# Other steps for the weight conversions beside an attention, other places for sums and remainders in the layers behind it

## The chip, the cores and the metric

The kernel runs on one core of a Trainium2 chip. Its time is the device time of one execution in microseconds, lower is better. Engines: PE is TensorE's matmul, PEld its weight load, DVE is VectorE, ACT is ScalarE, POOL is GpSimd, SP issues the DMAs. A conversion of a weight piece, a normalisation or a copy all run on one engine's queue in program order; an engine waits where an instruction's inputs or its output buffer are not free.

## The reference

Three layers follow each other. An attention (2 batches, 8 heads, 576 tokens, head size 64) with a bias that depends on positions, then a feed-forward layer, then 8 experts that are all computed for every token and summed with balanced weights.

```
scores = q @ k.T / 8 + bias[h, i, j]
attn = exp(scores - max) / sum;  x = attn @ v            # 1152 tokens x 512
h = x @ w_in;  g = softplus(h);  x = g @ w_out           # 512 -> 2048 -> 512
P = balanced(exp(x @ w_gate))                            # 8 rounds of rows and columns
out = sum over e of P[:, e] * (relu(x @ w1[e]) @ w2[e])  # 512 -> 1024 -> 512, e < 8
```

w_in and w_out arrive as 64 bit floats, everything else as 32 bit.

## The kernel before, in words

**The attention** walks over 8 pairs (batch, two heads). Each pair has nine steps, one for each tile of 128 query rows and head (five row tiles, some of them shared between the two heads). Step s runs 0 to 71; `r = s % 9` is the step's place in its round. In step s TensorE transposes the probabilities of step s - 3 (`transp`), computes the scores of step s + 1 (`qk`, two PSUM buffers) and multiplies older probabilities with v (`pv`), in an order that a table sets for each r. DVE adds the bias and takes the maximum (`soft`, L397), ACT takes the exponential (L401), and ACT or POOL normalises (`norm`, L409 and L411). `prep` makes the next pair's query and key operands in some of the steps (DVE casts at L293, POOL remainders at L332 and L343). At the end of each step `beside(s)` issues work of the next layer.

**Operands in two parts.** Matmuls run on a rounded high part and its remainder, three products for each: hi*hi, lo*hi, hi*lo. So every operand is split by one ACT copy and one subtraction on DVE or POOL. Weights: `parts` (L637 ACT, L638 POOL), called as "high" for a unit's up weights and "highd" for its down weights. Activations: L684, L660, L745 for the high part; L661, L747, L749 for the remainder.

**Conversions.** A piece of a 64 bit weight is loaded into a `raw` buffer and becomes 32 bit in a tile of `fs` in four steps: m (`rescale`, L602 ACT and L603 POOL), a (`convert_a`, L608 DVE), b (`convert_b`, L613 DVE), c (`convert_c`, L619 DVE). A unit has four pieces, two for the up weights, two for the down weights. For unit 0 the table EARLY gives, for each piece, the steps of its load, m, a, and b with c; ESPLIT the steps of "high" and "highd". Two `raw` buffers are there during the attention, so a piece's load waits for c of the piece two before it. For the later units a list (`todo`) is worked off by `convert(n)` in fixed places of the unit before.

**The units.** A unit is 256 columns of the hidden layer: the feed-forward layer has 8 (u < U1 = 8), the experts 32. A unit's up part makes z for two halves of 512 tokens (c) and two column blocks (f); 128 last tokens are computed apart (`up_last`, `turn_last`, `down_last`). Units 0, 1 and 8 do it plainly (`plain`, 12 matmuls for each z); the others by seven products in Strassen's manner (`product`, in the order 1, 2, 6, 5, 7, 3, 4), which need sums of the token blocks, S1 to S4 (`first_sum`, `first_split` in units 0 and 1), and sums of weights (`mix`). The products accumulate in three PSUM banks X ("t"), Y ("tail") and Z ("pv"); copies v1, u2, u3 keep what a bank held (`keep`, L729), and `add` (L724) makes z out of a bank and a copy. Then `act` or `rest_of` run softplus (L742, L777) and the split (L745, L747, L749). `down(u, c)` makes four chunks of tokens out of h and adds each to `acc` (`evac`, L848 on ACT in unit 0, L850 on DVE after it); acc lies in the buffers in which the attention's result x lay. `down_last` does it for the last tokens in the bank "pv", which product 5 of the next unit needs.

Z of unit 0's first two products lies in one PSUM tile of two banks (`pool["z"]`); DRAIN issues these products and the first softplus beside the last attention steps. The order of work on each engine is the program's own: nothing reorders it.

Of the kernel before, what the change touches and what calls it, by code (L numbers as in the profile page):

```python
# [70 lines left out]

EARLY = ((10, 14, 16, 19), (12, 20, 22, 25), (30, 36, 38, 41), (34, 42, 44, 47), (42,), (48,))
ESPLIT = ((28, "high", 0), (50, "highd", 0))
XAT = ((67, "A11", 0), (68, "A11", 1), (70, "A12", 0), (71, "A12", 1), (72, "A21", 0), (73, "A21", 1))

DRAIN = ((72, "up", (0, 0)), (74, "act", (0, 0)), (74, "up", (0, 1)))

# [15 lines left out]
def attention_moe_moe_kernel(ctx: ExitStack, tc, qT, kT, vN, wpos, w_in, w_out, w_gate, e_w1, e_w2,  # L93
# [439 lines left out]
    def experts(m0, accp, xr):  # L533
# [46 lines left out]
        def whole2(u, k):  # L580
            return fs[(0 if u == 0 else 3 + u % 2) if k else 2 * (u % 2)]

# [123 lines left out]

        def plain(u, c, f):

            if u == 0 and c == 0:
                if f == 0:  # L710
                    pool["z"] = ps2("z")
                zz = pool["z"][:, f]
            else:
                zz = bank(("t", "t", "tail", "pv")[2 * c + f] if u < U1 else "t")
            z[c, f] = zz
            for k in range(KT):
                for n, (a, b) in enumerate(TRIPS):
                    o = 256 * k + 128 * f
                    nc.tensor.matmul(zz, wu(u)[:, a, o:o + 128], xs[f"A{c + 1}{k // 2 + 1}"][b][k % 2],  # L719
                                     start=(k == 0 and n == 0), stop=(k == 3 and n == 2))  # L720

        def add(u, bank_, name):
            out = hold[bank_ if u >= U1 and name != "u3" else name]
            nc.vector.tensor_tensor(out=out, in0=hold[bank_], in1=hold[name], op=ALU.add)  # L724
            return out
# [28 lines left out]
        def low():  # L754
            while lows:
                lows.pop(0)()
# [313 lines left out]
        def unit(u):  # L1070
# [13 lines left out]
            if u < U1:  # L1084
# [4 lines left out]
                elif u in PLAIN:  # L1089
                    for n, (c, f) in enumerate(((0, 0), (0, 1), (1, 0), (1, 1))):  # L1090
                        do(u, (c, f))
                        low()
                        act(u, c, f, z[c, f])
                        if n == 1:
                            weights["highd"](u, 0)
                            first_split("S4")
                        convert(2)
                        jobs(n)
                    up_last(u)
                    low()  # L1100
                else:
                    for n, p in enumerate(UP):
# [13 lines left out]
                jobs(8)  # L1116
                turn_last(u)
                down(u, 1)
                if u == 0:
                    first_split("S2")  # L1120
                convert(len(todo))
                if u == 1:
                    first_split("S3", nc.vector)
                down_last(u)
                load_down()
# [60 lines left out]
        def first_plain():  # L1186

            def up(c, f):
                do(0, (c, f))
                low()  # L1190
                act(0, c, f, z[c, f])

            tmp = [pool["moe"].tile([128, 512], F32, tag=t, bufs=1, name=t) for t in ("v1", "u2", "u3", "s3")]
            pool["tmp"] = dict(S1=tmp[0:2], S2=[fs[1][:, 0:512], fs[1][:, 512:1024]], S3=tmp[2:4], S4=tmp[0:2])
            up(0, 0)
            first_sum("S1")
            low()
            first_sum("S2")
            up(0, 1)
            first_split("S1")  # L1200
            low()
            first_sum("S3")
            up(1, 0)
            first_sum("S4")
            up(1, 1)
            low()
            up_last(0)

# [132 lines left out]
```

## Time and profile before

| | |
|---|---|
| median of 3 runs | 1234.54 us (1233.07 to 1234.57) |
| the profiled execution's own time | 1233.09 us |
| its span, first to last instruction | 1231.3 us |
| mean granted TensorE clock | 0.992 |
| busy: PE, PEld | 96%, 81% |
| busy: DVE, ACT, POOL | 63%, 46%, 48% |

The position bias is built in the first 95 us; the attention's first bias add is at 100.3 us, its last at 258.5; unit 0's down part begins at 280, unit 2 at 319, the experts at 465. In the rows below times are counted from the span's start. A busy time is that of an engine's instructions; an idle time in brackets stands ahead of the instruction that it is printed with, and the name behind it is what the profile takes to have ended it.

### The profile page before, as it was taken

The numbers are of one execution on the slowest core, as the hardware profiler recorded it, in microseconds if no ns is written. First come the engines' busy times: TensorE is split into PE (matmuls) and PEld (weight loads), VectorE is DVE, ScalarE is ACT, GpSimd is POOL, SyncE is SP. The second block draws the span as 40 slices with busy tenths as digits, with TensorE's granted clock in tenths as the row PEclk, the third lists the DMA queues.
The fourth block names the chain that finished last, engine by engine and source line by source line (L and its number), as shares of the span: only waits on it lengthen the run. The fifth ranks groups of instructions, "written<-read, shape, count | busy, mean of one in ns | idle before, by whom it ended". The sixth has DMA issues, their size and how long they took to land.

```text
span 1231.3 us, 19016 instructions
## 1 busy us (share of the span) xinstructions
PE 1179.1 (96%) x7418; PEld 996.8 (81%) x7418; DVE 774.1 (63%) x1372; ACT 567.7 (46%) x987; POOL 591.5 (48%) x477
## 2 busy tenths in 40 slices
PE   5877999999999999999999999999999999999998
PEld 4776888888788877888888888888888888888887
DVE  8996778648888867466545555555554554554554
ACT  7976677767445554334334224224323323323421
POOL 0115676646787893434534534534533543543440
PEclk9898999999999999999999999999999999999999
DMA  3577566202222320111111111111111111111002
GB/s 101 169 209 209 171 194 181 83 35 87 86 73 100 103 69 18 52 35 52 52 35 52 52 35 45 58 36 35 54 50 35 52 52 35 52 52 35 35 1 77
DMA packets 58573, 90.86 MB, mean 74 GB/s; under 512 B 6900, under 2 KB 37236, under 8 KB 58484
## 3 DMA queue, kind: packets, MB, share of 16 engines
q1 hardware_dynamic: 58196, 89.35, 23.1%
q8 instruction: 58, 0.95, 0.3%
q10 hardware_dynamic: 288, 0.30, 0.1%
q14 instruction: 31, 0.25, 0.1%
HBM read 74.45 MB, written 15.19 MB: 73 GB/s over the span
## 4 chain that ended last, share of the span: by engine, by line
PE 84%; DVE 9%; ACT 3%; issue 1%; DMA 1%; POOL 1%; SPq 0%; DVEq 0%; POOLq 0%; ACTq 0%
PE sum L817 36%; PE t L703 15%; PE pv L703 8%; PE tail L791 4%; PE pv L833 4%; PE tail L703 4%; PE op L472 3%; PE sps L384 2%; PE tp L435 2%; PE t L719 1%; ACT m L197 1%; DVE m L200 1%; PE pac L210 1%; DVE extra L234 1%; DMA raw<-in_kT_dram 1%
## 5 line engine op out<-in xcount | busy, mean ns | idle before, releaser
L638 POOL TENSOR_TENSOR wu<-f,wu 128x1024 fp32r<-128x1024 f32 x77 | 186.3, 2419 | 410.1 <-ACT wu L637 409.3
L817 PE MATMUL sum<-wd,h 128*128 128x512 f32 x1536 | 364.7, 393 | 0.0
L817 PEld LDWEIGHTS sum<-wd,h 128*128 128x128 f32 x1536 | 283.3, 188 | 56.3
L852 DVE SCALAR_TENSOR_TENSOR acc<-sum,prob,acc 128x512 f32<-128x512 f32 x224 | 168.2, 751 | 146.5 <-PE sum L817 146.5
L703 PE MATMUL t<-room,wu 128*128 128x512 f32 x592 | 164.5, 389 | 0.0
L729 ACT ACTIVATE v<-t 128x512 f32<-128x512 f32 x37 | 22.2, 599 | 244.6 <-PE t L703 244.6
L703 PEld LDWEIGHTS t<-room,wu 128*128 128x128 f32 x592 | 111.1, 188 | 23.5 <-DVE u L724 0.3
L703 PE MATMUL pv<-x,wu 128*128 128x512 f32 x444 | 113.8, 392 | 2.5 <-DVE acc L850 2.4
L638 POOL TENSOR_TENSOR wd<-f,wd 128x1024 fp32r<-128x1024 f32 x40 | 96.5, 2414 | 11.3 <-ACT wd L637 10.5
L703 PEld LDWEIGHTS pv<-x,wu 128*128 128x128 f32 x444 | 82.6, 188 | 21.5 <-DVE acc L850 4.2
L637 ACT ACTIVATE wu<-f 128x1024 fp32r<-128x1024 f32 x77 | 81.0, 1053 | 29.9 <-POOL f L634 23.8
L210 PE MATMUL pac<-bw,m 128*128 128x64 bf16 (+1 forms) x1920 | 68.5, 200 | 27.2 <-ACT m L197 13.4
L817 PE MATMUL sum<-h,wd 128*128 128x512 f32 x384 | 91.6, 393 | 1.5 <-DVE h L749 0.8
L210 PEld LDWEIGHTS <-m 128*128 128x128 bf16 (+1 forms) x1920 | 65.2, 105 | 30.3 <-issue 17.7
L703 PE MATMUL t<-x,wu 128*128 128x512 f32 x296 | 85.1, 389 | 0.0
L817 PEld LDWEIGHTS sum<-h,wd 128*128 128x128 f32 x384 | 70.5, 188 | 17.1 <-ACT acc L848 1.5
L745 ACT ACTIVATE hl<-tail 128x256 fp32r<-128x256 f32 x40 | 15.5, 386 | 141.8 <-PE tail L800 141.8
L724 DVE TENSOR_TENSOR u<-t,u 128x512 f32<-128x512 f32 x37 | 25.6, 692 | 72.4 <-PE t L703 69.8
L850 DVE TENSOR_TENSOR acc<-sum,acc 128x512 f32<-128x512 f32 x80 | 55.0, 688 | 22.9 <-PE sum L817 22.1
L703 PEld LDWEIGHTS t<-x,wu 128*128 128x128 f32 x296 | 55.6, 188 | 11.5
L724 DVE TENSOR_TENSOR tail<-tail,v 128x512 f32<-128x512 f32 x31 | 21.7, 700 | 67.7 <-PE tail L703 67.7
L401 ACT ACTIVATE p<-p,sm 128x576 f32<-128x576 f32 x72 | 55.6, 772 | 17.4 <-DVE sm L397 14.4
(224 smaller groups left out, 2116.6 us busy)
## 6 DMA issues: line engine op xcount, KB each, us to landing
f<-in_e_w_dram SPq DMA_DIRECT2D x128, 256.0 KB, 2.8
bias<-wt SPq DMA_DIRECT2D x16, 576.0 KB, 5.8
raw<-in_w_in_dram SPq DMA_DIRECT2D x16, 512.0 KB, 3.6
raw<-in_w_out_dram SPq DMA_DIRECT2D x16, 512.0 KB, 3.5
wt<-extra SPq DMA_DIRECT2D x10, 512.0 KB, 4.4
raw<-in_qT_dram SPq DMA_DIRECT2D x16, 288.0 KB, 4.3
raw<-in_kT_dram SPq DMA_DIRECT2D x16, 288.0 KB, 4.4
vr<-in_vN_dram SPq DMA_DIRECT2D x8, 448.0 KB, 4.8
```

What stands on the lines that cost most here:

```text
L210: nc.tensor.matmul(pt[0:n, g], lhs, win(w, (k * (ng + 1) + gw) * NC, [[(ng - gw) * NC, 2], [1, NC]]), start=(k == 0), stop=(k == 2))
L401: nc.scalar.activation(p, p, AF.Exp, bias=sm[:, o:o + 1], scale=-1.0, accum_out=sm[:, 2 + o:3 + o])
L472: nc.tensor.matmul(op[:, 0:n], l, r, start=(part == 0 and k == 0), stop=(part == 8))
L637: nc.scalar.activation(w[:, 0], src, AF.Copy)
L638: nc.gpsimd.tensor_tensor(out=w[:, 1], in0=src, in1=w[:, 0].bitcast(F32), op=ALU.subtract)
L703: nc.tensor.matmul(zz, wu(u)[:, a, o:o + 128], xs[xn][b][j], start=(n in (1, 2, 5) and k == 0), stop=(k == 5), skip_group_check=True)
L724: nc.vector.tensor_tensor(out=out, in0=hold[bank_], in1=hold[name], op=ALU.add)
L791: nc.tensor.matmul(zr[:, 0:256], xl[:, b, k], wu(u)[:, a, 256 * k:256 * k + 256], start=(n == 0), stop=(n == 3 * KT - 1))
L817: nc.tensor.matmul(s, lhs, rhs, start=(n == 0), stop=(n == 5))
L833: nc.tensor.matmul(r, t[:, b, 128 * f:128 * f + 128], w[:, a, f], start=(n == 0), stop=(n == 5))
L850: nc.vector.tensor_tensor(out=d, in0=o, in1=d, op=ALU.add)
L852: nc.vector.scalar_tensor_tensor(out=d, in0=o, scalar=pool["prob"][:, t, e:e + 1], in1=d, op0=ALU.mult, op1=ALU.add)
```

## The change

1. EARLY: m, a, and b with c of unit 0's four pieces move to other steps, all four pieces to the same three places of a round (8, 2, 3). The last two pieces' loads move two steps ahead, unit 1's second one two steps back.
2. ESPLIT: "high" and "highd" of unit 0 move from steps 28 and 50 to 63 and 72. For that the down weights of unit 0 lie in `fs[1]`, no longer in the up weights' `fs[0]`.
3. DRAIN: the second z product is issued ahead of the first softplus.
4. Unit 0's plain products of c = 1 are cut into two halves of the contraction, A21's for both f, then A22's. S4 is summed behind the remainders of h, into `fs[0]`.
5. The splits of S1, S2 and S4 move: S1 from unit 0's up part to the end of unit 1's, S2 ahead of unit 0's second down half, S4 from the middle of unit 1 behind that half.
6. `down_last` comes ahead of the conversions that are left in `todo` (and ahead of the S3 split in unit 1).
7. `add`: in the feed-forward layer product 3's sum stays in the PSUM bank; before it went to the SBUF tile u2.

```diff
-EARLY = ((10, 14, 16, 19), (12, 20, 22, 25), (30, 36, 38, 41), (34, 42, 44, 47), (42,), (48,))
-ESPLIT = ((28, "high", 0), (50, "highd", 0))
+EARLY = ((10, 17, 20, 21), (12, 26, 29, 30), (28, 35, 38, 39), (32, 44, 47, 48), (42,), (50,))
+ESPLIT = ((63, "high", 0), (72, "highd", 0))
...
-DRAIN = ((72, "up", (0, 0)), (74, "act", (0, 0)), (74, "up", (0, 1)))
+DRAIN = ((72, "up", (0, 0)), (74, "up", (0, 1)), (74, "act", (0, 0)))
...
         def whole2(u, k):
-            return fs[(0 if u == 0 else 3 + u % 2) if k else 2 * (u % 2)]
+            return fs[(1 if u == 0 else 3 + u % 2) if k else 2 * (u % 2)]
...
-        def plain(u, c, f):
+        def plain(u, c, f, ks=range(4)):
...
-            else:
+            elif ks[0] == 0:
                 zz = bank(("t", "t", "tail", "pv")[2 * c + f] if u < U1 else "t")
+            else:
+                zz = z[c, f]
             z[c, f] = zz
-            for k in range(KT):
+            for k in ks:
...
         def add(u, bank_, name):
-            out = hold[bank_ if u >= U1 and name != "u3" else name]
+            out = hold[name if name == "u3" or (u < U1 and name == "v1") else bank_]
...
                         if n == 1:
                             weights["highd"](u, 0)
-                            first_split("S4")
                         convert(2)
                         jobs(n)
                     up_last(u)
                     low()
+                    first_split("S1")
...
                 turn_last(u)
+                if u == 0:
+                    first_split("S2")
                 down(u, 1)
                 if u == 0:
-                    first_split("S2")
+                    first_split("S4")
+                down_last(u)
                 convert(len(todo))
                 if u == 1:
                     first_split("S3", nc.vector)
-                down_last(u)
                 load_down()
...
             def up(c, f):
-                do(0, (c, f))
                 low()
                 act(0, c, f, z[c, f])
...
             up(0, 1)
-            first_split("S1")
+            for ks in ((0, 1), (2, 3)):
+                for f in range(2):
+                    plain(0, 1, f, ks)
             low()
             first_sum("S3")
             up(1, 0)
-            first_sum("S4")
             up(1, 1)
             low()
+            first_sum("S4")
             up_last(0)
```

Three places in the engines' rows show it. First DVE in the attention, around b and c (L613, L619) of unit 0's first piece; L397 is the bias add of a step, L415 a remainder of transposed probabilities, L421 a copy of them, L293 the cast of the next pair's keys. Before:

```order
L407 RECIPROCAL sm<-sm 128x1
L613 SCALAR_TENSOR_TENSOR f_2555<-raw_2557,f_2555 128x512
L619 SCALAR_TENSOR_TENSOR f_2555<-raw_2557,f_2555 128x512
L397 ISA p,sm<-sps,bias 128x576
L397 ISA sm 128x1
L421 COPY po<-tp 128x4x128
L421 COPY po<-tps 128x320
L406 TENSOR_SCALAR sm<-sm 128x1
```

And of the change:

```order
L415 TENSOR_TENSOR pt<-tp,pt 128x4x128
L407 RECIPROCAL sm<-sm 128x1
L613 SCALAR_TENSOR_TENSOR f_2555<-raw_2557,f_2555 128x512
L619 SCALAR_TENSOR_TENSOR f_2555<-raw_2557,f_2555 128x512
L397 ISA p,sm<-sps,bias 128x576
L397 ISA sm 128x1
L415 TENSOR_TENSOR pt<-tp,pt 128x4x128
L407 RECIPROCAL sm<-sm 128x1
L293 CAST ks<-raw 128x1152
```

The pair stood ahead of the bias add of the round's step 2; now it stands two bias adds later, ahead of that of step 4, behind which the key cast comes.

Next TensorE at the attention's end: z is unit 0's second product, op the last products with v, tail and pv unit 0's products of c = 1 (room is A21 and the high part of A22, x_4613 the remainder of A22). Before:

```order
L472 MATMUL op<-pt,vx 128x320 x6
L719 MATMUL z<-room,wu_2553 128x512 x12
L472 MATMUL op<-po,vr 128x320 x5
L719 MATMUL tail<-room,wu_2553 128x512 x7
L719 MATMUL tail<-x_4613,wu_2553 128x512
L719 MATMUL tail<-room,wu_2553 128x512 x2
```

And of the change:

```order
L472 MATMUL op<-pt,vx 128x320 x6
L721 MATMUL z<-room,wu_2553 128x512 x12
L472 MATMUL op<-po,vr 128x320 x5
L721 MATMUL tail<-room,wu_2553 128x512 x6
L721 MATMUL pv<-room,wu_2553 128x512 x6
L721 MATMUL tail<-room,wu_2553 128x512
L721 MATMUL tail<-x_4613,wu_2553 128x512
```

z keeps its place on TensorE (what moved is ACT's softplus, which is now issued behind it); twelve matmuls that need only A21 now stand ahead of the first that needs A22.

Last DVE at the end of unit 1: acc<-pv adds the last tokens, L608, L613 and L619 convert unit 2's last piece, L1220 is the S3 remainder, L724 the first z of unit 2. Before:

```order
L850 TENSOR_TENSOR acc<-sum,acc 128x512
L608 TENSOR_SCALAR f_4603<-f_4603 128x512
L613 SCALAR_TENSOR_TENSOR f_4603<-raw_4606,f_4603 128x512
L619 SCALAR_TENSOR_TENSOR f_4603<-raw_4606,f_4603 128x512
L1220 TENSOR_TENSOR room<-u_4631,room 128x512
L1220 TENSOR_TENSOR room<-s_4632,room 128x512
L850 TENSOR_TENSOR acc<-pv,acc 128x512
L724 TENSOR_TENSOR v_5014<-tail,v_5014 128x512
```

And of the change:

```order
L852 TENSOR_TENSOR acc<-sum,acc 128x512
L608 TENSOR_SCALAR f_4603<-f_4603 128x512
L852 TENSOR_TENSOR acc<-pv,acc 128x512
L613 SCALAR_TENSOR_TENSOR f_4603<-raw_4606,f_4603 128x512
L619 SCALAR_TENSOR_TENSOR f_4603<-raw_4606,f_4603 128x512
L1226 TENSOR_TENSOR room<-u_4631,room 128x512
L1226 TENSOR_TENSOR room<-s_4632,room 128x512
L726 TENSOR_TENSOR v_5014<-tail,v_5014 128x512
```

The add of the last tokens moved ahead of four instructions, not of the first of the three conversions; the first z of unit 2 stands behind the same work as before.

## Rows read from the trace of the kernel before

**Rows 1.** Windows, one round each: stretch, length, engines' busy us (count), clock, DMA share, GB/s

```profile
119.24:138.26 19.02, 18.73 (x131) 16.93 (x130) 14.53 (x46) 14.89 (x35) 12.84 (x17) 1.00 0.82 254
138.26:161.68 23.42, 21.14 (x135) 18.66 (x134) 19.08 (x50) 14.96 (x36) 14.62 (x17) 0.93 0.37 107
161.68:180.93 19.25, 17.67 (x123) 16.02 (x122) 14.11 (x45) 15.07 (x35) 14.84 (x17) 1.00 0.66 206
180.93:201.87 20.94, 19.68 (x136) 17.54 (x135) 17.91 (x48) 15.68 (x36) 14.10 (x19) 1.00 0.54 157
201.87:223.48 21.61, 19.33 (x123) 17.02 (x123) 15.85 (x47) 14.88 (x34) 16.49 (x19) 0.95 0.68 218
223.48:242.26 18.78, 18.78 (x132) 17.67 (x131) 14.40 (x44) 14.34 (x33) 11.10 (x14) 0.97 0.21 58
242.26:260.24 17.98, 17.98 (x130) 16.56 (x128) 12.49 (x41) 15.69 (x38) 8.72 (x13) 1.00 0.01 1
```

**Rows 2.** TensorE's waits, 100 to 320 us: total, times, longest

```profile
PE sps L384 <- DVE sm L397: 6.5, 5, 2.6
PE tp L435 <- POOL p L411: 4.9, 8, 1.9
...
PE sum L817 <- ACT acc L848: 0.7, 1, 0.7
PE z L719 <- ACT z L742: 0.7, 1, 0.7
PE tail L719 <- DVE x L661: 0.3, 1, 0.3
```

**Rows 3.** Tile f, 95 to 262 us: ns min/median/max, first and last start

```profile
L613 DVE SCALAR_TENSOR_TENSOR f<-raw,f x4: 673/968/1266, 141.3 to 207.2; 128x512 int32<-128x512 int32 x4
L619 DVE SCALAR_TENSOR_TENSOR f<-raw,f x4: 1116/1453/1801, 142.6 to 207.9; 128x512 int32<-128x512 int32 x4
```

**Rows 4.** Windows from bias add to bias add: steps 41, 59, 47 to 49, 56 to 58

```profile
192.16:196.11 3.95, 3.95 (x32) 3.88 (x32) 3.88 (x8) 2.81 (x6) 3.64 (x3) 1.00 0.01 2
235.14:236.11 0.97, 0.97 (x10) 0.97 (x9) 0.94 (x6) 0.67 (x2) 0.75 (x1) 1.00 0.00 0
204.81:212.67 7.86, 7.86 (x55) 7.06 (x53) 7.21 (x18) 5.59 (x14) 5.28 (x7) 1.00 0.61 152
227.14:235.14 8.00, 8.00 (x55) 7.19 (x54) 6.08 (x16) 5.40 (x14) 4.79 (x7) 1.00 0.47 131
```

**Rows 5.** Timeline of DVE behind step 3 of P6: start, us, instruction, idle before

```profile
231.93 0.76 DVE L397 CUSTOM_DVE_ANT_0 p<-sps,bias 128x576 f32<-128x576 f32 x1 [0.76 <-PE sps L384]
...
233.00 0.69 DVE L415 TENSOR_TENSOR pt<-tp,pt 128x512 fp32r<-128x512 f32 x1 [0.30 <-ACT pt L414]
...
234.08 1.13 DVE L293 CAST ks<-raw 128x1152 fp32r<-128x1152 f32 x1 [0.33 <-DMA raw<-in_kT_dram]
```

**Rows 6.** TensorE's waits, 318 to 470 us

```profile
PE pv L703 <- DVE acc L850: 2.4, 2, 2.0
PE sum L817 <- DVE h L749: 0.8, 1, 0.8
```

**Rows 7.** Timeline of DVE and of ACT in unit 0, 281 to 283 us

```profile
281.10 1.78 DVE L1214 TENSOR_TENSOR s<-xr 128x512 f32<-128x512 f32 x1
...
282.99 0.60 ACT L848 ACTIVATE acc<-sum 128x512 f32<-128x512 f32 x1 [0.70 <-PE sum L817]
```

**Rows 8.** Timeline of DVE, ACT and PE between units 1 and 2, 318 to 328 us

```profile
318.09 2.63 DVE L608 TENSOR_SCALAR f<-f 128x512 int32<-128x512 int32 x1
...
324.15 0.68 DVE L850 TENSOR_TENSOR acc<-pv,acc 128x512 f32<-128x512 f32 x1
...
326.66 0.58 ACT L729 ACTIVATE u<-pv 128x512 f32<-128x512 f32 x1
...
327.73 0.62 PE L703 MATMUL pv<-x,wu 128*128 128x512 f32 x2
```

**Rows 9.** Timeline of DVE in unit 7

```profile
450.54 2.36 DVE L749 TENSOR_TENSOR h<-u,h 128x512 fp32r<-128x512 f32 x1 [1.36 <-ACT h L745]
```

More of the change, by code (lines that the diff above doesn't have):

```diff
@@ L712, in plain @@
                 zz = pool["z"][:, f]
+            elif ks[0] == 0:
+                zz = bank(("t", "t", "tail", "pv")[2 * c + f] if u < U1 else "t")
             else:
-                zz = bank(("t", "t", "tail", "pv")[2 * c + f] if u < U1 else "t")
+                zz = z[c, f]
             z[c, f] = zz
-            for k in range(KT):
+            for k in ks:
                 for n, (a, b) in enumerate(TRIPS):
@@ L1193, in first_plain @@
             tmp = [pool["moe"].tile([128, 512], F32, tag=t, bufs=1, name=t) for t in ("v1", "u2", "u3", "s3")]
-            pool["tmp"] = dict(S1=tmp[0:2], S2=[fs[1][:, 0:512], fs[1][:, 512:1024]], S3=tmp[2:4], S4=tmp[0:2])
+            pool["tmp"] = dict(S1=tmp[0:2], S2=[fs[1][:, 0:512], fs[1][:, 512:1024]], S3=tmp[2:4],
+                               S4=[fs[0][:, 0:512], fs[0][:, 512:1024]])
             up(0, 0)
```

## The prediction

> **What bounds the kernel now.** TensorE is busy for 96% of the span, so only two things can shorten it: the stretches in which TensorE waits, and those in which its clock is low. I looked for both by stage. The windows over the attention come first: from the second round on I cut them at the start of the bias add (L397) of each round's first step, so a window is one round of nine steps; call them P1 to P7 [rows 1]. The reader should see that the same work takes 17.98 us in P7, which has neither weight conversions nor the preparation of a next pair, and 18.78 in P6, which has the preparation but no conversion; P6 ran at a mean granted clock of 0.97, that is partly at the lower level after a wait of TensorE, and 18.78 x 0.97 = 18.2. So a round costs about 18.2 when nothing disturbs it. P1 to P5, which carry the conversions, take 19.02, 23.42, 19.25, 20.94 and 21.61, and P2 shows a clock of 0.93. TensorE's waits say by whom: for DVE's bias add (6.5 us, the first of them in the start-up round) and for GpSimd's normalisation (4.9) [rows 2]. The rest of the attention and the first two units hold three waits of 0.7, 0.7 and 0.3; the units after them 2.4 and 0.8 [rows 2, 6]. From there to the end TensorE hardly waits, and the change does not touch that part.
>
> **The conversions in the attention.** One piece is m (ACT, then GpSimd), a (DVE, L608), b and c (DVE, L613 and L619). The order is: before, b and c stand in the rounds' steps 1, 7, 5 and 2 (counted from 0), after the change always behind step 3, a always behind step 2, m behind step 8. What each old place cost:
> - Step 5 (s = 41, in P4): 3.95 us from bias add to bias add where P6 has 0.97, so 3.0 [rows 4]. P4 is 2.7 above 18.2, so this pair is all of it: P4's two m and two a, in four different steps, cost nothing measurable. I cost m and a at nothing in their new places too; they hide in ACT's and DVE's idle time (busy 14.34 and 14.40 of P6's 18.78 [rows 1]).
> - Step 2 (s = 47, in P5): three steps took 7.86, in P6 8.00 [rows 4]: nothing. P5's 3.4 above 18.2 is then the split of the down weights ("highd", s = 50), which sat in GpSimd's queue ahead of a normalisation.
> - Steps 1 and 7 (P2): 5.2 together, the lower clock included.
> - The split "high" (s = 28) is all that P3 had: 1.05.
>
> What does the new place, step 3, cost? No row has b and c there. Behind it DVE has three idle spots before the next bias adds: 0.76 (waiting for TensorE's scores), 0.30 (for ACT) and 0.33 (for the key load), 1.4 in all [rows 5]. The pair takes 0.67 + 1.12 at its shortest and 0.97 + 1.45 at its median [rows 3], 1.8 to 2.4. So 0.4 to 1.0 us stay uncovered, and the scores' two buffers take up part of it. From below the bound is step 2's nothing, from above step 5's 3.0. I take 0.5, near the neighbouring step: 18.7 for each of P2 to P5.
>
> P1 loses a piece's a and keeps one m: 18.2. P6 no longer follows the long wait behind highd, so its clock is full: 18.2. P7 gets "high" at its first step: I charge what it cost in P3, 1.05, so 19.03 (from below nothing, since GpSimd has only 8.72 busy there). "highd" now stands behind the last softmax, between ACT's and GpSimd's halves of the x splits; what it delays (a copy to SBUF and A21's second remainder) is read some microseconds later, behind the second z product: nothing, at most 1. The loads move by a step or two on SP's queue, each behind the conversion that frees its buffer and none ahead of a key load that waits: nothing.
> New sum: 18.2 + 4 x 18.7 + 18.2 + 19.03 = 130.2. Old: 141.0 [rows 1]. **Gain 10.8.**
>
> **The first two units.** The second z product waited 0.7 for ACT's softplus of the first [rows 2]: both lie in one tile of two banks. Issued ahead of it, it waits for nothing, and the softplus has the time of that product and of the last ten op matmuls: gain 0.7. The two products of c = 1 now do their A21 halves first, so A22's remainders have 2.7 us more: gain 0.3 [rows 2]. The down product waited 0.7 for ACT's first acc [rows 2]. The row names TensorE as what held ACT up, but acc also overwrites x of A11, and the last S3 sum, which reads that x, ended at 281.10 + 1.78 = 282.88, just ahead of ACT's 282.99 [rows 7]: I read the sum as the true releaser. It took 1.78 while GpSimd ran the S1 split; an add of this size takes 0.68 in [rows 8]. The S1 split goes to the end of unit 1 and S4 behind the remainders, so the acc is free earlier: gain 0.7. The three splits that are placed anew issue as many instructions as before, behind or ahead of weights' splits that keep their places; nothing.
>
> **Behind the last tokens.** In unit 1, acc<-pv ended at 324.83, behind a, b, c and two S3 remainders; TensorE had waited 2.0 for its bank, since 322.8 [rows 6, 8]. Only a stays ahead of it, whose end is 320.72: the bank is free at 321.4, in time. But what DVE does next (v) still comes behind the same work. ACT's softplus of v waits for it, and behind that stands the copy u<-pv, which ends at 327.24 and which product 3 needs; product 3 began at 327.73 [rows 8]. So the wait comes back there, and of 2.0 I count 0.4. The same wait in unit 2 (2.4 - 2.0 = 0.4) I count in full, since its copy comes out just in time. Product 3's sum now stays in PSUM: in unit 7 DVE's remainder of it took 2.36 [rows 9], two operands from SBUF, while TensorE waited 0.8 [rows 6]; an add of the same shape with one operand in PSUM takes 0.68 [rows 8]. Gain 0.8; the longer hold of the bank ends before its next user, the last tokens' product. **Gains outside the attention: 0.7 + 0.3 + 0.7 + 0.4 + 0.4 + 0.8 = 3.3.**
>
> **Sum.** 10.8 + 3.3 = 14.1 off the profiled execution's own 1233.09 (a span of 1231.3 and 1.8 around it): 1219.0. That execution is at the low end of the runs shown, whose median is 1.45 higher; I give 1219.5 as the median to come.
>
> **Rivals.**
> - *GpSimd holds the pair up.* If GpSimd's normalisation runs when b starts, b and c take their longest, 1.27 + 1.80 [rows 3], as in step 5, where GpSimd was busy for 3.64 of 3.95 [rows 4]. Less 1.4 idle, 1.7 stay uncovered instead of 0.5: 4 x 1.2 = 4.8 more, 1224.3. For it: a normalisation is due in that step. Against: it is one short instruction, not the key remainders of step 5. Chance 0.15. The Trainium skill, "SBUF — State Buffer", section "Who interferes with whom", states just this: a VectorE instruction with two SBUF inputs and a GpSimd instruction that reads SBUF block each other for a whole instruction, whoever starts first. By that rule alone the sum would be this rival's; the 1.12 to 1.80 of c agree with it, but no row shows who would start first in step 3.
> - *The waits outside the attention only move.* As product 3's does; then 3.3 are missing: 1222.8. Against: four of the six have no second waiter that I found. 0.14.
> - *Step 3 is as dear as step 5.* 4 x 2.5 = 10 more: 1229.5. Against: step 5 had one bias add 0.97 behind the other, step 3 has 1.4 of idle behind it. 0.10.
> - *Slower.* Bias add and normalisation both come so late that TensorE stands in every round and its clock falls, as in P2. With 23.42 in each of the four rounds it is 4 x 4.7 = 18.9 more: 1238.4. It decides from 22.2 a round on, that is 4.0 for one pair, and the dearest pair in the trace cost 3.0. 0.03.
> - *Nothing changes*, because the old excess is the bias and key loads' (the DMA share is 0.66 in P3 and 0.82 in P1 [rows 1]): 1233 to 1235. Against: P3 has that load and only 1.05 of excess. 0.03.
>
> **Numbers.** The forecast case, 1215 to 1223, has 0.55. The range goes from 1213 (pairs and "high" free, 3 less, and some clock) to 1228, which takes in the first two rivals, also both together, and leaves out the third and the two after it. A difference under 0.2% (2.5 us) can't be told from none here. Faster 0.94, same 0.03, slower 0.03.
>
> **What would show it.** Right: P2 to P5 between 18.2 and 19.3 with a clock of 1.00; bias add to bias add behind step 3 about 1 us longer than P6's and the next ones no longer; no TensorE wait at z, tail and the first acc; a wait of about 1.5 at product 3 of unit 2; the remainder of 2.36 at 0.7. Wrong: rounds of 20 us or more; TensorE waiting for a normalisation three steps behind step 3; a clock under 1.00 in P7, which "high" would have caused.

## The result

| | before | changed |
|---|---|---|
| median of 4 runs | 1233.80 us (1230.01 to 1234.57) | 1220.03 us (1219.45 to 1221.02) |
| the profiled execution's own time | 1233.09 us | 1221.02 us |
| its span | 1231.3 us | 1219.2 us |
| mean granted TensorE clock | 0.992 | 0.996 |

The ratio is 0.9894, with a 95% interval of 0.988 to 0.9909: faster by 1.1%. The forecast was 1219.5.

First the rounds of the attention, cut as in [rows 1] (the columns are the same): P1 to P6 from bias add to bias add, P7 to the first z product.

```profile
120.11:138.32 18.21, 18.21 (x129) 16.70 (x128) 14.11 (x45) 14.43 (x35) 12.04 (x16) 1.00 0.82 250
138.32:159.62 21.30, 19.25 (x132) 17.28 (x131) 16.44 (x47) 14.99 (x35) 13.27 (x17) 1.00 0.45 114
159.62:178.56 18.94, 18.89 (x131) 16.95 (x130) 16.23 (x49) 15.10 (x36) 13.35 (x17) 1.00 0.72 226
178.56:197.42 18.86, 18.82 (x129) 16.88 (x129) 16.16 (x48) 15.04 (x35) 13.32 (x17) 1.00 0.50 147
197.42:216.35 18.93, 18.90 (x131) 16.93 (x130) 16.20 (x48) 15.13 (x35) 13.34 (x17) 1.00 0.70 217
216.35:234.82 18.47, 18.45 (x130) 16.87 (x129) 14.02 (x45) 14.43 (x33) 12.05 (x16) 1.00 0.40 121
234.82:253.37 18.55, 18.19 (x128) 16.31 (x126) 12.49 (x41) 16.69 (x39) 11.08 (x14) 1.00 0.01 1
```

The clock is 1.00 in every round. P3 to P5 come out at 18.86 to 18.94 (before 19.25, 20.94, 21.61), P7 pays 0.57 for "high". P2 is the exception: 21.30, of which TensorE is busy for 19.25. Together the rounds lost 7.7 us, where the prediction had 10.8. This execution's first round began 0.87 later than that of before (the start-up does the same work), so at the first z product 6.9 are left. The 21.30 is a round of over 20, which the prediction had named as a sign of being wrong; what it is worth is taken up below.

TensorE's waits from 100 to 320 us, which answer to [rows 2]; from 318 to 470 us, where [rows 6] had two kinds of wait, the row at product 3 is all there is:

```profile
PE sps L384 <- DVE sm L397: 7.5, 4, 3.2
PE pv L703 <- ACT u L731: 1.2, 1, 1.2
PE tp L435 <- ACT p L409: 1.0, 3, 0.4
```

Gone are the waits for GpSimd's normalisation (4.9), at sum, at z and at tail (0.7, 0.7, 0.3), one of 1.9 for a DVE copy in P2 that [rows 2] leaves out, and, behind 318, those for DVE's acc and for its remainder in unit 7. New are 1.66 in P2, which lie in the first row (the rest of that row is the first round's, 5.8, before 5.6), and product 3's wait of 1.25 in unit 2, where about 1.5 was forecast.

Behind the attention I cut the time at the starts of TensorE's last-token products (`down_last`), one in each unit:

| stretch | before | changed | gained | forecast |
|---|---|---|---|---|
| first z product to first down product | 19.81 | 18.25 | 1.56 | 1.0 |
| unit 0's down part | 12.38 | 11.19 | 1.19 | 0.7 |
| unit 1 | 24.86 | 25.23 | -0.37 | 0 |
| unit 2 | 25.76 | 25.06 | 0.70 | 0.4 |
| unit 3 | 24.30 | 23.49 | 0.81 | 0.4 |
| units 4, 5, 6 | 71.31 | 70.77 | 0.54 | 0 |
| unit 7 | 24.75 | 23.76 | 0.99 | 0.8 |
| together | | | 5.42 | 3.3 |

6.9 and 5.4 make the 12.1 that the spans differ by, but for 0.2 that is lost again behind unit 7. The medians differ by 13.8; the table's parts are those of two executions. Two lines of the table are more than a size: the gain in unit 0 and the loss in unit 1. First unit 0, DVE's second S3 sum and ACT's first add to acc, which answer to [rows 7]:

```profile
272.17 0.68 DVE L1220 TENSOR_TENSOR s<-xr 128x512 f32<-128x512 f32 x1
...
273.32 0.61 ACT L850 ACTIVATE acc<-sum 128x512 f32<-128x512 f32 x1
```

The sum takes 0.68 (before 1.78), and the acc behind it waits for nothing. In unit 1 three rows, DVE's c, GpSimd's S2 split and up-weight remainder (wu), and TensorE's first products:

```profile
279.44 1.66 DVE L619 SCALAR_TENSOR_TENSOR f<-raw,f 128x512 int32<-128x512 int32 x1
...
278.78 3.49 POOL L1226 TENSOR_TENSOR x<-f,x 128x512 fp32r<-128x512 f32 x2 [1.70 <-ACT x L1225]
282.28 2.53 POOL L638 TENSOR_TENSOR wu<-f,wu 128x1024 fp32r<-128x1024 f32 x1
...
284.17 5.98 PE L721 MATMUL t<-room,wu 128*128 128x512 f32 x24
```

The S2 split, moved ahead of unit 0's second down half, runs on GpSimd in front of unit 1's wu, and beside c, which takes 1.66 instead of 0.69 like the c before it; wu is ready at 284.81, 0.6 behind the start of the products that read it, and the 24 matmuls take 5.98, in the kernel before 5.60.

Last the place between units 1 and 2, as in [rows 8]: DVE's last-token add and v, ACT's softplus of v and its copy u<-pv, TensorE's product 3.

```profile
311.22 0.68 DVE L852 TENSOR_TENSOR acc<-pv,acc 128x512 f32<-128x512 f32 x1
...
315.06 0.68 DVE L726 TENSOR_TENSOR v<-tail,v 128x512 f32<-128x512 f32 x1
...
315.77 0.63 ACT L779 ACTIVATE v<-v 128x512 f32<-128x512 f32 x1 [1.44 <-DVE v L726]
...
316.97 0.58 ACT L731 ACTIVATE u<-pv 128x512 f32<-128x512 f32 x1
...
317.61 1.66 PE L703 MATMUL pv<-x,wu 128*128 128x512 f32 x6 [1.25 <-ACT u L731]
```

The add of the last tokens is in time, as forecast; v, still behind the same work, holds ACT for 1.44, and the copy behind the softplus holds TensorE for 1.25.

### The profile page after: what moved, and what is told of

Read it like the earlier page. It is cut to its first block, busy times and chain, and to the rows that moved or that the text cites. A ratio compares the mean times of both kernels' runs of the same rounds, so it can differ in the third digit from the quotient of the medians.

```text
span 1219.2 us, 19021 instructions
## 1 busy us (share of the span) xinstructions
PE 1172.5 (96%) x7418; PEld 992.5 (81%) x7418; DVE 769.6 (63%) x1372; ACT 568.4 (47%) x987; POOL 591.3 (48%) x477
## 4 chain that ended last, share of the span: by engine, by line
PE 81%; DVE 7%; DMA 4%; ACT 3%; POOL 2%; issue 2%; SPq 0%; DVEq 0%; POOLq 0%; ACTq 0%
PE sum L819 35%; PE t L703 16%; PE pv L703 8%; PE tail L793 4%; PE pv L835 4%; PE tail L703 4%; DMA raw<-in_kT_dram 2%; PE op L472 2%; PE t L721 1%; ACT m L197 1%; DVE m L200 1%; POOL ql L332 1%; DMA raw<-in_qT_dram 1%; DVE extra L234 1%; PE sps L384 1%
## 5 line engine op out<-in xcount | busy, mean ns | idle before, releaser
L638 POOL TENSOR_TENSOR wd<-f,wd 128x1024 fp32r<-128x1024 f32 x40 | 96.4, 2410 | 10.8 <-ACT wd L637 10.0
L210 PE MATMUL pac<-bw,m 128*128 128x64 bf16 (+1 forms) x1920 | 65.3, 197 | 30.3 <-DVE extra L234 13.9
L210 PEld LDWEIGHTS <-m 128*128 128x128 bf16 (+1 forms) x1920 | 62.0, 103 | 33.5 <-issue 20.8
```

Source lines behind the costliest of these rows:

```text
L210: nc.tensor.matmul(pt[0:n, g], lhs, win(w, (k * (ng + 1) + gw) * NC, [[(ng - gw) * NC, 2], [1, NC]]), start=(k == 0), stop=(k == 2))
L638: nc.gpsimd.tensor_tensor(out=w[:, 1], in0=src, in1=w[:, 0].bitcast(F32), op=ALU.subtract)
```

## Experiments

The theory after the result: the gain has two independent parts, the attention's steps (7 to 8 us) and the order behind it (5 to 6), and what is missing in the attention is P2's alone, a wait for a load. Rivals: the parts hang together; the place of b and c in the round doesn't matter, only that a place exists; the moved waits cost as much as they gave.

**Steps alone.** The kernel before, with the new EARLY, ESPLIT and `fs[1]`:

```diff
-EARLY = ((10, 14, 16, 19), (12, 20, 22, 25), (30, 36, 38, 41), (34, 42, 44, 47), (42,), (48,))
-ESPLIT = ((28, "high", 0), (50, "highd", 0))
+EARLY = ((10, 17, 20, 21), (12, 26, 29, 30), (28, 35, 38, 39), (32, 44, 47, 48), (42,), (50,))
+ESPLIT = ((63, "high", 0), (72, "highd", 0))
...
-            return fs[(0 if u == 0 else 3 + u % 2) if k else 2 * (u % 2)]
+            return fs[(1 if u == 0 else 3 + u % 2) if k else 2 * (u % 2)]
```

> The kernel before with the new steps of the conversions and of the two weight splits alone (edits 1 and 2, with the down weights in fs[1]). If the two groups of edits add up, the attention gives what the two profiles show up to the first z product (260.24 to 253.37: 6.9 us) and nothing behind it: about 1227 us, and the waits of 0.7 at z, 0.7 at the first acc and 2.0 at unit 2's bank stay. Rival: the gain in the attention is partly lost behind it, because the x sums and splits of unit 0 then come into the way sooner: 1229 to 1231, with longer waits in units 0 and 1.

Measured: 1226.65 us (1224.07 to 1227.87), ratio 0.9935 (0.9913 to 0.9956). Its first z product came 8.0 earlier than that of before, not 6.9, but units 2 and 3, whose code is unchanged, took 27.38 and 23.58 where before had 25.76 and 24.30.

**All but the steps.** The changed kernel with the old two tables:

```diff
-EARLY = ((10, 17, 20, 21), (12, 26, 29, 30), (28, 35, 38, 39), (32, 44, 47, 48), (42,), (50,))
-ESPLIT = ((63, "high", 0), (72, "highd", 0))
+EARLY = ((10, 14, 16, 19), (12, 20, 22, 25), (30, 36, 38, 41), (34, 42, 44, 47), (42,), (48,))
+ESPLIT = ((28, "high", 0), (50, "highd", 0))
```

> The changed kernel with the old tables EARLY and ESPLIT: only the edits outside the attention remain. If the groups add up: the attention's rounds as in the kernel before (P2 23.4, P4 20.9, P5 21.6) and the 5.2 us that the two profiles show behind the first z product: about 1228.5 us. Rival: these edits need the earlier end of the attention's conversions; then less than 3 us, 1231 or more.

Measured: 1226.82 us (1225.86 to 1230.39), ratio 0.9943 (0.9924 to 0.9963). The rounds were not those of before, 23.42 and 21.61, although the tables are the same; P2 and P5:

```profile
140.30:162.33 22.03, 19.45 (x134) 17.61 (x134) 19.14 (x50) 15.15 (x36) 14.61 (x17) 1.00 0.39 113
...
202.49:222.93 20.44, 18.33 (x124) 16.23 (x124) 15.80 (x47) 14.80 (x34) 15.42 (x18) 1.00 0.75 232
```

TensorE waited here at least as long as before, ahead of the same two groups of matmuls, 2.17 for a DVE copy in P2 and 1.89 for the normalisation behind "highd" in P5 (before 1.88 and 1.87). But the clock stayed at 1.00, where in the kernel before it fell to 0.57 behind P2's wait (145.75 to 148.00), near its lower level: the six matmuls behind that wait took 1.88 here and 3.31 there. P1 to P7 are 137.8, not 141.0. So about 3.2 of the old rounds' time were the price of a lower clock, which one execution of these tables paid and another did not.

The first run takes 8.0 us off its kernel before (1234.63, same chip), the second 7.8, and 15.8 is 2.0 over the whole change's 13.8, within what the intervals leave open: the parts add up as far as that can be told, and each alone gives about half.

**P2's load.** The changed kernel, with the second piece's load at step 19 instead of 12. In P2 DVE had stood before its cast of the next pair's queries, and TensorE before the next scores; these are the changed kernel's two rows:

```profile
142.69 0.76 DVE L293 CAST qh<-raw 128x1152 fp32r<-128x1152 f32 x1 [2.43 <-DMA raw<-in_qT_dram]
...
144.18 0.53 PE L384 MATMUL sps<-ks,qh 128*128 128x288 f32 x2 [1.66 <-DVE sm L397]
```

The query load was issued at 134.51, behind nine others between 125.32 and 130.00, and its data came some 8 us later. In the kernel before the cast ran at 139.73 without a wait on a load issued at 133.68.

```diff
-(12, 26, 29, 30)
+(19, 26, 29, 30)
```

> The changed kernel with the load of the second weight piece at step 19, no longer at step 12. Theory: in P2 DVE waits 2.4 us for the next pair's queries because their load stands behind two piece loads of 512 KB on the DMA engines; without one of them that wait goes, P2 falls from 21.3 to about 19 and the time to about 1217.7. Rival: the bias reads alone fill the DMA engines at that time; the queries land as late, P2 stays at 21 and the time at 1220.

Measured: 1219.54 us (1218.97 to 1219.65), ratio 0.988 (0.9858 to 0.9902); P2 18.82, P3 19.63 instead of 18.94. The wait in P2 is gone, but in P3 smaller ones stand, of DVE for the next query load (0.61) and of TensorE for a normalisation (0.40). The medians differ by 0.5 us and the ratios by 0.0014, or 1.7 us, both less than the intervals can tell apart. P2's wait is not always 2.43: in the eight other kernels here that keep b and c at step 3 and the load at 12, P2 took 18.79 to 19.72. So the profile of the changed kernel shows a bad draw of a wait whose usual price, against the 18.9 of P3 to P5, is 0 to 0.8.

**Another place for the pair.** The changed kernel with b and c behind step 5 of the rounds:

```diff
-EARLY = ((10, 17, 20, 21), (12, 26, 29, 30), (28, 35, 38, 39), (32, 44, 47, 48), (42,), (50,))
+EARLY = ((10, 17, 20, 23), (12, 26, 29, 32), (28, 35, 38, 41), (32, 44, 47, 50), (42,), (50,))
```

> The changed kernel with b and c of all four pieces behind step 5 of the round, no longer behind step 3. By the prediction's reading (step 5 cost 3.0 where step 3 costs 0.5): 4 x 2.5 = 10 more, 1230 us, rounds P2 to P5 about 2.5 longer, and b with c at 1.25 and 1.8 us beside GpSimd's key remainders. Rival: any step does, since DVE is idle for 2 to 4 us of every round, and only the places of the two weight splits cost time: 1220 to 1221.

Measured: 1225.33 us (1224.51 to 1225.88), ratio 0.9926 (0.9907 to 0.9945); P2 21.20, with a wait of 1.03 for the query load, P3 to P5 20.48, 20.33, 20.43. Tile f's b and c (ns min/median/max), first the changed kernel's, then this one's:

```profile
L613 DVE SCALAR_TENSOR_TENSOR f<-raw,f x4: 665/666/677, 147.9 to 204.7; 128x512 int32<-128x512 int32 x4
L619 DVE SCALAR_TENSOR_TENSOR f<-raw,f x4: 1116/1117/1117, 148.7 to 205.4; 128x512 int32<-128x512 int32 x4
```

```profile
L613 DVE SCALAR_TENSOR_TENSOR f<-raw,f x4: 1250/1259/1266, 152.0 to 213.2; 128x512 int32<-128x512 int32 x4
L619 DVE SCALAR_TENSOR_TENSOR f<-raw,f x4: 1789/1792/1795, 153.3 to 214.5; 128x512 int32<-128x512 int32 x4
```

The place sets the price to within some 20 ns, four times out of four. What it is at step 3 is seen in the changed kernel's rows of DVE and GpSimd in P3:

```profile
166.85 0.67 DVE L613 SCALAR_TENSOR_TENSOR f<-raw,f 128x512 int32<-128x512 int32 x1
167.55 1.12 DVE L619 SCALAR_TENSOR_TENSOR f<-raw,f 128x512 int32<-128x512 int32 x1
...
167.03 1.10 POOL L411 TENSOR_SCALAR p<-p,sm 128x576 f32<-128x576 f32 x1 [0.54 <-DVE sm L407]
```

b starts 0.18 ahead of the normalisation and runs at full speed; the normalisation takes 1.10 instead of its median of 0.75, c then 1.12 instead of 0.69. Each loses some 0.4 to the one that was first. At step 5 GpSimd is in the key remainders (two, 3.24 together, from 151.25), b starts at 151.97, and b and c lose 0.6 and 1.1. The Trainium skill, "SBUF — State Buffer", section "Who interferes with whom", states that a VectorE instruction with two SBUF inputs and a GpSimd instruction that reads SBUF contend, and that the second one to issue is blocked until the first has finished. These rows agree with it within some 0.15: 0.49 of b was left when the normalisation began, which lost 0.35, and 0.58 of that when c began, which lost 0.43. Per round the pair costs 1.5 more at step 5 than at step 3 by the rounds' lengths, where the prediction had 2.5 (3.0 less 0.5).

**Edit 7 undone:** product 3's sum goes to SBUF again.

```diff
-            out = hold[name if name == "u3" or (u < U1 and name == "v1") else bank_]
+            out = hold[bank_ if u >= U1 and name != "u3" else name]
```

> The changed kernel with product 3's sum in the SBUF tile u2 again (edit 7 undone). Theory: DVE's remainder of it has two SBUF operands again and is held up while GpSimd subtracts the down weights; in unit 7 it takes 2.4 us again and TensorE waits 0.8 for it, so from unit 6's last tokens to unit 7's it is 24.7 us, no longer 23.8; in the other units nothing. Rival: the bank's place costs or saves nothing, what ended the wait of unit 7 was the earlier end of acc<-pv; then 23.8.

Measured: 1221.95 us (2 runs), ratio 0.9898 (0.9878 to 0.9918); unit 7 took 26.79 instead of 23.76, the other units as in the changed kernel within 0.1. In the changed kernel the remainder of product 3's sum is this one:

```profile
439.08 0.69 DVE L751 TENSOR_TENSOR h<-pv,h 128x512 fp32r<-128x512 f32 x1 [1.28 <-ACT h L747]
```

Here, that remainder, GpSimd's splits beside it and the two TensorE waits of unit 7:

```profile
439.18 2.55 DVE L751 TENSOR_TENSOR h<-u,h 128x512 fp32r<-128x512 f32 x1 [1.36 <-ACT h L747]
...
436.41 4.78 POOL L638 TENSOR_TENSOR wd<-f,wd 128x1024 fp32r<-128x1024 f32 x2
...
435.43 1.66 PE L703 MATMUL pv<-x,wu 128*128 128x512 f32 x6 [1.63 <-ACT u L731]
...
441.79 4.40 PE L819 MATMUL sum<-h,wd 128*128 128x512 f32 x18 [0.97 <-DVE h L751]
```

The wait of 0.97 is the term (forecast 0.8, and 0.99 by the units' table). The other, 1.63 at product 3, was not expected: a c took 2.80 there, from 430.17, beside a GpSimd split that had begun at 430.02, and v came late. Whether undoing the edit brings that about or this execution alone had it, one profile doesn't tell; with the sum in SBUF and the old order of the last tokens (the kernel before and the run with the steps alone) unit 7 took 24.75 both times, with no wait there.

**Edit 6 undone:** `down_last` behind the conversions.

```diff
-                down_last(u)
                 convert(len(todo))
                 if u == 1:
                     first_split("S3", nc.vector)
+                down_last(u)
```

> The changed kernel with the last tokens behind the left over conversions again (edit 6 undone). Theory: TensorE waits 2.0 us at product 5 of unit 2 for the bank and no longer 1.25 at product 3, and about 0.4 and 0.1 in units 3 and 5: between the last tokens of units 1 and 2 it is about 25.8 us where the changed kernel has 25.1, and 24.3 to units 3 where it has 23.5. Rival: the 1.25 at product 3 come on top, 27 us.

Measured: 1221.07 us (2 runs), ratio 0.9891 (0.9871 to 0.9911); unit 2 took 27.20, the rival's number, not 25.8. TensorE's product 5 in the timeline, and the window behind it (columns as in [rows 1], the clock is the third number from the end):

```profile
313.03 2.55 PE L703 MATMUL pv<-x,wu 128*128 128x512 f32 x6 [1.80 <-DVE acc L852]
```

```profile
313.50:316.00 2.50, 2.50 (x8) 1.90 (x7) 1.10 (x3) 1.65 (x3) 1.02 (x1) 0.50 0.01 3
```

The wait of 1.80 is back at product 5, product 3 does not wait in addition; but behind the wait the clock is 0.50, the lower level, and 12 matmuls take 4.81 where they took 3.04. So the rival had the number by another cause: the wait and 1.8 of clock. That is not the old wait's price every time. The same wait in the run with the steps alone, then in the kernel before:

```profile
317.30 1.80 PE L703 MATMUL pv<-x,wu 128*128 128x512 f32 x6 [2.00 <-DVE acc L850]
318.89 2.76 PE L703 MATMUL t<-room,wu 128*128 128x512 f32 x6
```

```profile
324.88 1.66 PE L703 MATMUL pv<-x,wu 128*128 128x512 f32 x6 [1.99 <-DVE acc L850]
326.37 1.52 PE L703 MATMUL t<-room,wu 128*128 128x512 f32 x6
```

Behind 2.00 the granted clock fell (0.65 from 317.90 to 320.40) and the unit took 27.38; behind 1.99 it stayed at 1.00 and the unit took 25.76. So edit 6 is worth 0.7 in unit 2 where the clock holds and 2.1 to 2.3 where it falls. Units 4 to 6 took 71.36 without it (before 71.31, with it 70.77): 0.5 more is its own. The medians show 1.0 of this and the ratios nothing (0.9891 against 0.9894), with two runs against four.

**S2's split later.** The changed kernel with the S2 split in unit 1 behind "highd", away from unit 1's wu:

```diff
                             weights["highd"](u, 0)
+                            first_split("S2")
...
-                if u == 0:
-                    first_split("S2")
                 down(u, 1)
```

> The changed kernel with the split of S2 in unit 1 behind highd, no longer ahead of unit 0's second down half. Theory: there it stands on GpSimd ahead of unit 1's up weights and holds up c of their last piece, which ACT's half of that split waits for; TensorE's first products of unit 1 take 0.4 us longer than 24 matmuls need. Without it they do not, and unit 1 takes 24.85 us where the changed kernel has 25.2. Rival: the conversions' own length sets when the weights are there; unit 1 stays at 25.2.

Measured: 1220.91 us (1218.80 and 1223.02), ratio 0.989 (0.9863 to 0.9916); unit 1 at 25.33, not 24.85. TensorE's first products and first down products, and DVE's a and b beside the split:

```profile
281.93 5.70 PE L721 MATMUL t<-room,wu 128*128 128x512 f32 x24
...
294.33 6.02 PE L819 MATMUL sum<-h,wd 128*128 128x512 f32 x24
...
292.62 1.42 DVE L608 TENSOR_SCALAR f<-f 128x512 int32<-128x512 int32 x1
294.07 1.67 DVE L613 SCALAR_TENSOR_TENSOR f<-raw,f 128x512 int32<-128x512 int32 x1
```

The products' wait is nearly gone (5.70, before 5.60), but the split now meets a and b (1.42 and 1.67), the adds to acc come late, and the first down products take 6.02 where they took 5.63. That the split made those products late is confirmed, for 0.28 of the 0.37; the cure moves the loss.

**ACT's copy ahead of the softplus.** The delayed softplus runs behind product 5, not 6, in every unit:

```diff
-            if n in (6, 4):
+            if n in (5, 4):
```

> The changed kernel with the softplus of the second product's z behind the copy u3, no longer ahead of it (the held work runs after product 5, not 6). Theory: product 3 of unit 2 waits 1.25 us for that copy only because ACT's queue has the softplus ahead of it, which waits for DVE's v; the wait goes and unit 2 takes 23.8 us, no longer 25.1; the other units stay within 0.1. Rival: the softplus then comes too late for the remainder on GpSimd and the down weights behind it, and the wait comes back at the down products: unit 2 at 24.5 to 25, units 3 to 6 0.3 to 0.6 longer each.

Measured: 1229.14 us (1228.11 to 1229.66), ratio 0.9954 (0.9937 to 0.997). Unit 2 took 24.17 instead of 25.06, units 3 to 6 each 25.97 or 25.98, 2.2 to 2.5 more. In unit 3, GpSimd's wd remainder, DVE's c, and the longest of TensorE's waits:

```profile
341.52 2.40 POOL L638 TENSOR_TENSOR wd<-f,wd 128x1024 fp32r<-128x1024 f32 x1
...
341.73 2.74 DVE L619 SCALAR_TENSOR_TENSOR f<-raw,f 128x512 int32<-128x512 int32 x1
...
348.83 3.02 PE L819 MATMUL sum<-h,wd 128*128 128x512 f32 x12 [1.59 <-DVE acc L852]
```

ACT's later softplus moves GpSimd's remainder to 0.2 ahead of DVE's c, which then takes 2.74 (1.55 in the changed kernel, where the remainder began 1.4 ahead of it). The rest of DVE's unit is late, to the adds to acc. The rival was right that units 3 to 6 pay, and far too small; in unit 2 itself 24.17 lies between the two.

**The same in unit 2 alone:**

```diff
-            if n in (6, 4):
+            if n in ((5, 4) if u == 2 else (6, 4)):
```

> The changed kernel, but unit 2 alone runs the delayed softplus and split behind product 5 (the units after it behind product 6, as before), so that ACT's copy u<-pv isn't queued behind a softplus that waits for DVE's v. Theory (the order is right only where v comes late, which is in unit 2 alone): from unit 1's last tokens to unit 2's 24.2 us instead of 25.06, no TensorE wait at product 3 of unit 2, units 3 to 7 as in the changed kernel (23.5, 23.8, 23.5, 23.8): 0.9 us less, 1219.1, of which the medians may show little. Rival (the later softplus moves the remainders of h of unit 2 into the next unit's products, so its price comes there): unit 3 at 24.0 or more, 1220 to 1221.

Measured: 1218.93 us (1218.63 to 1222.47), ratio 0.9884 (0.9859 to 0.9908). Unit 2 took 24.18 and units 3 to 7 23.50, 23.52, 23.81, 23.52, 23.77: the theory's numbers. ACT's copy in unit 2 waits only for its product:

```profile
313.38 0.60 ACT L731 ACTIVATE u<-pv 128x512 f32<-128x512 f32 x1 [0.70 <-PE pv L703]
```

**Both cures,** unit 2's order and the load at 19:

> The changed kernel with two edits: unit 2's order as in the run beside it, and the second piece's load at step 19 instead of 12, which takes away DVE's wait for the query load in the second round. If both hold: second round 18.8, third 18.9 to 19.6, unit 2 at 24.2, together 1 to 2 us under the changed kernel: 1218.5, ratio to the kernel before 0.987 to 0.988. Rival: what the load gains comes back in the third round, and unit 2's in unit 3; then 1220, and nothing to tell it from the changed kernel.

Measured: 1218.31 us (1217.75 to 1221.92), ratio 0.9875 (0.9854 to 0.9897), the lowest of all. P2 18.60, P3 18.98, unit 2 24.20. The stages do what was expected; 1.7 us from the changed kernel's median is less than the two ratios' intervals can tell apart.

**z's order undone:**

```diff
-DRAIN = ((72, "up", (0, 0)), (74, "up", (0, 1)), (74, "act", (0, 0)))
+DRAIN = ((72, "up", (0, 0)), (74, "act", (0, 0)), (74, "up", (0, 1)))
```

> The changed kernel with the old order of z (first softplus ahead of the second product). From the first z product to the first down product: 18.25 us in the changed kernel, 19.81 in the kernel before. If the term of the prediction is right, the wait of 0.7 at z comes back and 18.25 becomes 18.95; the other 0.9 of the difference belongs to the halved products of the second token half and to the sums and splits moved away. Rival: all of the difference is z's (its wait also delays the softplus and the remainders behind it): 19.7 or more.

Measured: one run, 1220.33 us; first z product to first down product 19.56, so 1.3 of the 1.56 are z's order, of which this row has 1.04 as the wait (1.03 in the run with the steps alone, 0.67 before: the new steps make the old order dearer):

```profile
258.33 3.03 PE L721 MATMUL z<-room,wu 128*128 128x512 f32 x12 [1.04 <-ACT z L744]
```

**S1's split back in unit 0's up part:**

```diff
             up(0, 1)
+            first_split("S1")
...
                     low()
-                    first_split("S1")
```

> The changed kernel with the S1 split back in unit 0's up part (ahead of the products of the second token half), no longer at the end of unit 1's. If GpSimd's split is what made DVE's S3 sums long and held ACT's first add to acc: an S3 sum of 1.2 to 1.8 instead of 0.68, TensorE waiting 0.5 to 0.9 for ACT's acc again, from the first down product to the last tokens' 11.9 us or more instead of 11.2. Rival (the sum was not what released acc; the products' new order made TensorE's wait go): 11.2 to 11.3, whatever the sums take. Unit 1 may gain back some of the 0.4 that it lost.

Measured: one run, 1222.37 us; unit 0's down part 13.03 instead of 11.19, unit 1 26.51 instead of 25.23. DVE's S3 sums, ACT's acc, and TensorE's two waits:

```profile
270.20 1.80 DVE L1220 TENSOR_TENSOR u<-xr 128x512 f32<-128x512 f32 x1
271.92 1.77 DVE L1220 TENSOR_TENSOR s<-xr 128x512 f32<-128x512 f32 x1
...
273.81 0.60 ACT L850 ACTIVATE acc<-sum 128x512 f32<-128x512 f32 x1 [0.70 <-DVE s L1220]
...
274.46 3.29 PE L819 MATMUL sum<-h,wd 128*128 128x512 f32 x12 [1.30 <-ACT acc L850]
...
286.49 1.88 PE L721 MATMUL t<-room,wu 128*128 128x512 f32 x7 [1.23 <-POOL wu L638]
```

Here the trace itself names the S3 sum as what released acc, with TensorE behind it: the reading of [rows 7] was right. The sums' 2.2 us more also make b and c late, and with them unit 1's wu: its new wait grows from 0.4 to 1.2.

## Why the prediction was right

The total was right, 14.1 forecast and 13.8 by the medians, and the mechanism of most terms was shown. But not each part came as forecast: between the two profiled executions, 12.1 apart, the attention's rounds gave 7.7 of 10.8 and the units 5.4 of 3.3. That the two misses nearly cancel is luck.

Part of the attention's miss lies in the sum that the prediction took away from. The old rounds' 141.0 hold 3.2 of lower clock behind two waits, which the same tables did not pay in another execution (137.8). The new rounds, forecast at 130.2, took 133.3 in the changed kernel's profile and 130.7 to 132.0 in the eight other kernels with these steps. Where the clock holds, then, the steps are worth 5.8 to 7.1. How that divides between the conversions' steps and the two weight splits' is not shown, since EARLY and ESPLIT were undone only together.

- *Step 3 costs 0.5 for b and c.* Right within 0.2: P3 to P5 are 0.4 to 0.5 above this execution's P6 and 0.7 above the 18.2 that the prediction counted from. The pair took its shortest of before, 0.67 + 1.12, with b ahead of the normalisation. The rival that GpSimd holds the pair up had its condition (who starts first) right and fell on it.
- *Step 5 costs 3.0 a pair.* Too much: one step's excess was read as the round's. A round with the pair at step 5 lost 1.5 more than one at step 3, about 2.0 in all; later steps gave a part back: in P3 of that kernel step 5 took 3.96 from bias add to bias add (0.98 in its P6), but step 7 2.35 (3.45).
- *"high" costs 1.05 in P7.* 0.57, and 0.55 to 0.58 in every other kernel with the new steps; the visible wait is 0.36, for ACT's probabilities.
- *The loads' moves cost nothing.* This step failed. By the two profiles it is nearly all of the 3.1 that the attention is short (P2 has 2.6 of it), by the other executions the smaller part beside the old rounds' clock. The second piece's load did not move, but at its step it holds up a query load that DVE now waits for. Why in the kernel before it waited for none is not settled; P2's 18.79 to 19.72 in the eight other kernels says that a term of 0 to 0.8 was due.
- *z 0.7 and tail 0.3.* 1.56, of it 1.3 for z: the wait alone was 1.04 where it was brought back, more than the 0.7 of before. The other 0.26 fit the tail's 0.3, but edit 4 was not undone by itself.
- *The S3 sum holds acc, 0.7.* The mechanism was shown, the size was 1.19, and 1.84 in the run that undid it.
- *The three splits cost nothing.* Wrong for S2's: 0.37 in unit 1. It passed GpSimd's wu remainder in the queue, and beside it c took 1.66; I had looked at what the splits delay where they left, not where they arrive.
- *The wait between units 1 and 2 moves to product 3; 0.4 is left.* Right in place, with 1.25 for a forecast of about 1.5; the gain was 0.70. *Unit 2's wait, 0.4:* the table has 0.81 for unit 3, where it stood, but without edit 6 that unit took 23.64, 0.15 more than with it, and with the code of before in the run with the steps alone 23.58, without that wait. So the wait was that one execution's, and most of the 0.81 with it. The 0.54 of units 4 to 6, forecast at 0, is edit 6's, since it went when that was undone.
- *Product 3's sum in PSUM, 0.8.* 0.99, and the remainder takes 0.69 where it took 2.36 [rows 9].

## What to carry to other kernels

An instruction that must share SBUF with GpSimd has a price for its place, not for itself: look which instruction of GpSimd's starts within some tenths of a microsecond of it, before and after the move, and look for it where moved work arrives as well as where it left. Price a late step by its whole round, since part of a delay is given back later. Look at the clock behind a long wait, and at more than one execution before its price goes into a sum: the same wait cost 1.2 to 1.8 more in one and nothing in another. A cure for one unit (ACT's copy ahead of the softplus) gained 0.9 there and cost 10 in the five units behind it, which were in step already: apply it where the wait is.

## What was not expected of the hardware

- When GpSimd's remainder began 0.2 instead of 1.4 us ahead of DVE's c, c took 2.74 instead of 1.55; each of the four units in that kernel took 2.2 to 2.5 us more.
- After a wait of 1.80 TensorE ran at a clock of 0.50 for at least 2.5 us and lost 1.8 more; after the wait of 1.25 at product 3 it stayed at 1.00, and after P2's 1.66 too. The length of the wait alone does not decide it: the clock fell after 2.00, 1.88 and 1.87 and stayed at 1.00 after 1.99, 2.17 and 1.89, at the same three places of the program.
- A query load of 2 x 288 KB took some 8 us to land in one execution, where DVE waited 2.43 for it; in the eleven other kernels with the same loads ahead of it DVE waited between nothing and 1.03.
